# Holding the value and output weights behind the query and key weights of the second group

## The chip, the cores and the metric

The kernel runs on one core of a Trainium2 chip. The metric is the device time of one execution in microseconds (us). The core has five instruction streams that matter here: TensorE (PE, with its weight loads PEld) multiplies and transposes, VectorE (DVE) and ScalarE (ACT) move results out of the accumulator memory (psum) and do the elementwise work, GpSimd (POOL) does small copies, and SyncE (SP) issues all DMA transfers. Each stream runs its instructions in the order in which they were written and waits on semaphores for the others.

## The reference

Two layers, each a memory-augmented attention (A) and then a gated MLP (B), over 2048 tokens of width 448; both layers use the same weights. Attention walks over 64 segments of 32 tokens; 8 memory rows go in front of each segment and come out of it changed, so the segments form a recurrence.

```python
for s in range(n_seg):                       # 64 segments, one after the other
    h = concat([mem, x[:, s*32:(s+1)*32]])   # 8 + 32 rows
    q, k, v = h @ Wq, h @ Wk, h @ Wv         # 16 heads of 256
    p = softmax(where(mask, q @ k.T / 16, -1e9))
    o = sum_over_heads((p @ v) @ Wo)
    mem = o[:, :8]; outs.append(o[:, 8:])
# B: (relu(x @ W_gate) * (x @ W_up)) @ W_down
x = x + A(layernorm(x)); x = x + B(layernorm(x))   # twice
```

## The kernel before, in words

The kernel first folds weights: for each head A = Wq·Wkᵀ (scaled) and B = Wv·Wo, both kept in on-chip memory, so that the later work is per head a product with A, a softmax and a product with B. Folding needs the weights turned: TensorE transposes a loaded piece into psum (L742 for Wq and Wk, eight matmuls a turn; L747 for Wv), DVE or ACT copies it into one of seven buffers `WT`, and TensorE multiplies (L761).

The heads' query and key weights come in four groups, g = 0 to 3. Each group has four loads (query and key, two pairs of heads, here q0, k0, q1, k1), eight turns (each load has two halves, here called T30k1 for group 3, first half, k1) and fourteen products in two blocks of seven (A30, A31). There are only eight staging slots, so the loads of group 2 wait until group 0 has been turned, and those of group 3 until group 1 has. The loads of group 0 are cut in halves of 224 KB; the others have 448 KB.

Then there are eight loads of Wv (three transfers each, into slots 8 to 15) and eight of Wo. Half of Wv and Wo are folded at once (`values(0)`), half after the recurrence has gone two steps (`values(1)`). The first two steps work with unfolded Wv and Wo (`unfused`, L1039 and L1062) and need all of both.

The recurrence (`chain`) has 70 steps: layer 1's 63 and layer 2's, which follow 7 steps behind. A step multiplies the memory `mT` with A (L934), takes the softmax (`middle`), multiplies with B (L973), and turns the result into the next `mT` (L996 and L444). The attention of the other tokens (L1274, L1300, L451) and the MLP (L1372, L451) lie between the steps.

Every piece of work is an operation with its inputs and outputs, handed to a list scheduler (`_Sched`). Three things set the order: the dependencies; for SP, DVE, ACT and POOL a due time, shifted for each part of the program by a letter of the string `ORDER` (`part()`, a quarter step a letter, negative before the letter a); and for TensorE the string `LINE`, which picks in turn from the operations left, so that TensorE's order is fixed entirely by it. Where the scheduler's own clock expects TensorE to be idle for long, it puts in filler matmuls (L1406, a line of `spin`). An operation reads `r`, writes `w`; a name in `r` is waited for. DMA number n also waits for number n − 48.

## Time and profile before

| | us |
|---|---|
| median of 3 runs | 1504.0 (1503.89 to 1506.61) |
| profiled execution | 1502.79 |
| its span, first to last instruction | 1501.0 |
| granted TensorE clock, mean | 0.999 |
| TensorE busy | 1482.8 |

| stretch (us) | what it is |
|---|---|
| 0 to 62 | weights arrive and are folded; the recurrence begins at 57.55 (L934) |
| 62 to 100 | the first two steps with unfolded Wv and Wo (L1039 at 67.87 and 85.64), the rest of the folding |
| 100 to 1501 | recurrence, attention and MLP together; the MLP's weights are issued from 87.5 to 162.5 |

The profile gives each instruction's start and length; "idle before" is the time that its engine stood still ahead of it, and the arrow names the event that ended it. The granted clock is the share of full speed that TensorE's throttle let through.

### The profile page before, as it was taken

What the parts mean: (1) busy time and instruction counts of PE and PEld (TensorE: products, weight loads), DVE (VectorE), ACT (ScalarE), POOL (GpSimd) and SP (SyncE); (2) the same over time, 40 slices, a digit from 0 to 9 for tenths busy, and PEclk for the clock granted to TensorE, in tenths of its full rate; (3) what the DMA queues carried; (4) which work ended last, traced back from release to release, by engine and by line L of the source; (5) the groups of instructions that cost most, each with busy time, mean ns of one, the idle gap of its engine ahead of it and who ended that gap; (6) DMA issues with size and microseconds to landing.
All of it is one profiled execution on the core that took longest, in us unless ns stands there. A gap on an engine that the chain in (4) does not pass through costs nothing.

```text
span 1501.0 us, 83432 instructions
## 1 busy us (share of the span) xinstructions
PE 1482.8 (99%) x37128; PEld 1059.1 (71%) x37128; DVE 1144.8 (76%) x3528; ACT 909.7 (61%) x2539; POOL 171.7 (11%) x669
## 2 busy tenths in 40 slices
PE   8999999999999999999999999999999999999999
PEld 6557566676767777777768677777768776677776
DVE  6657678787777878688878877688777877778765
ACT  6776566666666666555565656565665665565543
POOL 3010111111111111011110111011110011111000
PEclk9999999999999999999999999999999999999999
DMA  9602100000000000000000000000000000000000
GB/s 231 184 25 66 54 7 12 11 9 8 9 4 12 11 8 15 4 17 6 17 6 12 11 9 14 3 18 5 18 5 8 14 9 14 4 10 6 12 5 15
DMA packets 62262, 34.12 MB, mean 23 GB/s; under 512 B 31552, under 2 KB 61776, under 8 KB 61904
## 3 DMA queue, kind: packets, MB, share of 16 engines
q1 hardware_dynamic: 61904, 28.80, 8.1%
q8 instruction: 292, 4.78, 1.4%
q14 instruction: 66, 0.54, 0.1%
HBM read 21.36 MB, written 1.84 MB: 15 GB/s over the span
## 4 chain that ended last, share of the span: by engine, by line
PE 94%; DVE 2%; ACT 1%; DMA 1%; issue 1%; SPq 0%; POOL 0%; DVEq 0%
PE psG L451 24%; PE psG L1274 17%; PE psG L1372 12%; PE psC L973 11%; PE psC L934 9%; PE psG L934 4%; PE psG L1185 3%; PE psG L761 3%; PE psG L1300 2%; PE psC L451 2%; PE psC L1128 2%; PE psC L1185 1%; PE psG L973 1%; PE psG L1188 1%; DMA Bsb<-in_A_Wq_dram 1%
## 5 line engine op out<-in xcount | busy, mean ns | idle before, releaser
L1274 PE MATMUL psG<-HT,A 64*128 64x128 bf16 x4980 | 288.9, 216 | 1.2 <-issue 1.2
L451 PE MATMUL psG<-Bsb,YT 128*128 128x448 bf16 x1288 | 274.6, 352 | 0.0
L1274 PE MATMUL psG<-HX,A 64*128 64x128 bf16 x3735 | 269.6, 216 | 0.5 <-issue 0.3
L1274 PEld LDWEIGHTS psG<-HT,A 64*128 64x128 bf16 x4980 | 236.5, 94 | 13.6 <-issue 4.2
L441 ACT ACTIVATE Ug<-psG 64x128 bf16<-64x128 f32 (+2 forms) x442 | 156.6, 374 | 68.5 <-PE psG L1274 56.6
L1274 PEld LDWEIGHTS psG<-HX,A 64*128 64x128 bf16 x3735 | 195.5, 94 | 0.8 <-issue 0.8
L1372 PE MATMUL psG<-G,glu 64*128 64x128 bf16 x5950 | 190.7, 216 | 1.2 <-issue 0.9
L1372 PEld LDWEIGHTS psG<-G,glu 64*128 64x128 bf16 x5950 | 175.4, 94 | 13.6 <-issue 6.2
L451 PEld LDWEIGHTS psG<-Bsb,YT 128*128 128x128 bf16 x1288 | 113.0, 97 | 95.7 <-issue 10.0
L973 PE MATMUL psC<-Bsb,YTm 128*32 128x448 bf16 x3416 | 172.9, 353 | 0.4
L1112 DVE STREAM_TRANSPOSE uT<-Usb 128x384 bf16<-128x384 bf16 x280 | 154.0, 551 | 0.8
L934 PE MATMUL psG<-A,mT 64*32 64x448 bf16 x4032 | 152.5, 350 | 0.0
L934 PE MATMUL psC<-A,mT 64*32 64x448 bf16 x3808 | 147.3, 350 | 0.5 <-ACT mT L441 0.5
L973 PEld LDWEIGHTS psC<-Bsb,YTm 128*32 128x32 bf16 x3416 | 85.5, 97 | 67.0 <-DVE YTm L444 1.6
L441 ACT ACTIVATE YT<-psG 128x448 bf16<-128x448 f32 x233 | 118.8, 543 | 10.6 <-PE psG L1188 9.1
L444 DVE CAST Ug<-psG 64x128 bf16<-64x128 f32 (+2 forms) x254 | 108.1, 438 | 16.9 <-PE psG L1274 12.9
L934 PEld LDWEIGHTS psC<-A,mT 64*32 64x32 bf16 x3808 | 76.0, 92 | 53.4 <-ACT mT L441 5.2
L1377 ACT ACTIVATE hG<-psG 128x512 bf16<-128x512 f32 (+1 forms) x127 | 69.0, 543 | 63.2 <-PE psG L1372 58.0
L451 PE MATMUL psG<-glu,hG 128*128 128x448 bf16 x448 | 99.3, 352 | 0.0
L934 PEld LDWEIGHTS psG<-A,mT 64*32 64x32 bf16 x4032 | 80.1, 92 | 19.8 <-DVE mT L444 0.7
L1378 DVE TENSOR_TENSOR hG<-hG,psG 128x512 bf16<-128x512 bf16 (+1 forms) x116 | 70.5, 613 | 29.2 <-ACT hG L1377 28.3
L444 DVE CAST YT<-psG 128x448 bf16<-128x448 f32 x136 | 82.0, 616 | 9.5 <-PE psG L1188 8.1
(235 smaller groups left out, 2856.9 us busy)
## 6 DMA issues: line engine op xcount, KB each, us to landing
HR<-xn SPq DMA_DIRECT2D x128, 32.0 KB
Tsb<-Rsb SPq DMA_DIRECT2D x256, 1.5 KB
Tsb<-Rsb SPq DMA_DIRECT2D x256, 2.0 KB
Bsb<-in_A_Wk_dram SPq DMA_DIRECT2D x6, 448.0 KB
Bsb<-in_A_Wq_dram SPq DMA_DIRECT2D x6, 448.0 KB
HR<-Rsb SPq DMA_DIRECT2D x126, 1.5 KB
HR<-Rsb SPq DMA_DIRECT2D x126, 2.0 KB
X<-in_A_x_dram SPq DMA_DIRECT2D x16, 112.0 KB
```

The costliest lines, as they stand in the source:

```text
L441: return E.activation(out, i, ACT.Copy, scale=1.0 if scale is None else scale)
L444: return E.tensor_copy(out, i)
L451: return E.matmul(out, lhsT=lhsT, rhs=rhs, **k)
L761: i = E.matmul(bk.ap()[row0:row0 + mn, to:to + of.stop - of.start], lhsT=lhs[:, et, m0:m0 + mn], rhs=rhs[:, et, of], start=(et == 0), stop ...
L934: i = E.matmul(ub[v].ap()[32 * j:32 * j + 32, 0:D], lhsT=self.mT[rw, WHERE[b], first:first + 32], rhs=cols, start=(b == 0), stop=(b == 6), ...
L973: x = E.matmul(bo.ap()[32 * j:32 * j + 32, 0:D], lhsT=self.YTm[:, q, :], rhs=self.Bsb[:, chunks[q], :], start=(i == 0), stop=(i == 13), ti ...
L1112: self.s.add("dve", 578, lambda E, e, out=out, hh=hh: E.transpose(out, heads[hh]), r=[("Usb", 2 * half + v) for v in range(2)], w=[f"uT{ha ...
L1185: return E.matmul(ps[:, n * q:n * q + n], lhsT=HR[rows, 128 * q:128 * q + 128], rhs=PT, start=True, stop=True, tile_position=(b, 0))
L1274: i = E.matmul(ub[v].ap()[:, 128 * n:128 * n + 128], lhsT=self.A[rw, b, a0:a0 + 128], rhs=HT[rw, WHOLE[b], :, 0:SEG] if CROSS[b] is None e ...
L1372: i_ = E.matmul(two[v].ap()[:, 128 * c:128 * c + 128], lhsT=self.Wgu[rw, b, f0:f0 + 128], rhs=G[rw, WHOLE[b] if CROSS[b] is None else 4 + ...
L1377: s.add("act", 170 + 0.833 * N, lambda E, e, dst=dst, z=two[0], N=N: E.activation(dst, z.ap()[:, 0:N], ACT.Relu), r=[two[0]], w=[("hG", i, ...
L1378: s.add("dve", dv_cost(N), lambda E, e, z=two[1], N=N, dst=dst: E.tensor_tensor(dst, dst, z.ap()[:, 0:N], ALU.mult), r=[two[1]], w=[("hG", ...
```

## The change

Three edits. First, each turn of query and key weights and of Wv counts itself and writes a name with its number, `("turned", n)`; the program adds the eight turns of a group one after the other, so number 16 is the last of group 1, T11k1. Second, every load of Wv and Wo reads `("turned", 16)`, so SP waits for that turn before it issues any of them. Third, `ORDER` and `LINE` are new strings of the same number of parts and operations.

```diff
-ORDER = ("AkAPMPZMEsWPzkVtwAm0YgdLXFCHdymsALTpcTXKWNMRKLt0H0AgHAG0gihNl0bCLbZBRyVqwoWAgOvEFplk0ptQ0orawUuaBIdaABka0AA0aa"
+ORDER = ("UmAPMPKcivEldPoriUbRkLTLNJGAf0xHXdoenVpAhHQfNEWvukAQBufSjhHCW0EXWAwAauKAwp0BxPPAAfdpsqrPwpYakozaLnIavdcaYoO0aa"
...
-LINE = ("AFGEENLEGEEEFEEEMIIFGFEEFFMEM~UIJHEEEEAEDGAGECCCCCECABIIICFBECCBBKJCDCEDCBCBJJIECFDDBBJMrBIMNIAEBCECCACADBaaCC"
+LINE = ("AEEFEMMEJHHGEEEEHGGEFEGGEEELLLHJFEFEEEAM~JLIGEFEEDDDKKEFDEFDDADAKBCBFBCBBACKBAIDABCABANBIAMNHECJADDCBAAcFBAZZB"
...
             self.dma(self.Wst[slot][:, 0:3, :], src[64:448, c0:c0 + 512].rearrange("(k p) c -> p k c", p=128), 393216,
-                     w=[("Wst", slot)])
-            self.dma(self.Wst[slot][0:64, 3, 0:256], src[0:64, c0:c0 + 256], 32768, w=[("Wst3", slot)])
-            self.dma(self.Wst[slot][64:128, 3, 256:512], src[0:64, c0 + 256:c0 + 512], 32768, w=[("Wst4", slot)])
+                     r=[("turned", 16)], w=[("Wst", slot)])
+            self.dma(self.Wst[slot][0:64, 3, 0:256], src[0:64, c0:c0 + 256], 32768, r=[("turned", 16)], w=[("Wst3", slot)])
+            self.dma(self.Wst[slot][64:128, 3, 256:512], src[0:64, c0 + 256:c0 + 512], 32768, r=[("turned", 16)], w=[("Wst4", slot)])
 
         def transposes(slot, hh, wt, rot):
             s.part()
+            turn[0] += 1
...
-            s.add("pe", ..., fn, r=keys + ["ident"], w=[bk], alloc=[bk], room=[("WT", wt)])
+            s.add("pe", ..., fn, r=keys + ["ident"], w=[bk, ("turned", turn[0])], alloc=[bk], room=[("WT", wt)])
...
-                self.dma(self.Wos[n][:, :, :], self.Wo_d[:, 4 * p:4 * p + 4, :], 458752, w=keys + homes[n])
+                self.dma(self.Wos[n][:, :, :], self.Wo_d[:, 4 * p:4 * p + 4, :], 458752, r=[("turned", 16)], w=keys + homes[n])
...
-                    self.dma(self.Wos[n][hh], ..., 229376, w=[keys[hh]] + homes[n])
+                    self.dma(self.Wos[n][hh], ..., 229376, r=[("turned", 16)], w=[keys[hh]] + homes[n])
```

Read against the order in which the program adds the operations, the two `LINE` strings give TensorE these orders up to the first step (Tg-half-load is a turn, A and B blocks of products, n0 and n1 the first tiles' transposes, U0 the first product of the recurrence, "mask" small setup matmuls):

```
before: T00k0 T00k1 T00q0 T00q1 T01q1 T01q0 A00 T01k0 T01k1 T10k0 A01 T10q1 T10k1 T11q0 T10q0 T11q1 n0 A10 mask
        T11k1 T11k0 A11(1) mask A11(6) T20q0 T20k1 T20k0 mask T20q1 T21q0 T21k0 T21q1 A20 T21k1 T30q1 T30k0 A21
        T30k1 T30q0 T31k0 T31q1 T31q0 A30 Tv00 Tv01 n1 T31k1 B00 B01 Tv10 B00 mask A31(3) B00 A31(3) B01 A31 B10 B0 U0
after:  T00q0 T00k0 T00k1 T00q1 T01k0 T01q1 A00 T01q0 T01k1 A01(6) T10k0 T10q1 A01(1) T10q0 T10k1 T11q0 T11k0 T11q1
        A10 T11k1 mask T20q1 n0 T20k0 A11 T20q0 T20k1 T21q0 T21k0 A20 mask T21k1 mask T30k0 T21q1 A21 mask
        T30k1 T31k0 T30q1 T30q0 T31q1 A30 Tv01 T31k1 Tv00 T31q0 B01 Tv10 B00 A31(2) B0 A31(2) B00 A31(3) B00 n1 Tv11 B01(2) U0
```

In the loads' part of `ORDER`, the first tile's x load goes from the letter A (6.5 steps early) to U (1.5 early). Group 1's loads stand at q0 0.75, k0 −3.75, q1 −0.75, k1 −5.25 before, and at −1.75, −3.75, −3.25, −4.25 after; group 3's at 0.25, −6.0, −3.75, 0.25 before, and at −5.5, −0.75, −1.0, −6.5 after (in steps, negative is earlier).

More of the change, by code (lines that the diff above doesn't have):

```diff
@@ L32 @@
 STEPS = "ABCDEFGHIJKLMNOPQRSTUVWXYZabcdefghijklmnopqrstuvwxyz0"
-ORDER = ("AkAPMPZMEsWPzkVtwAm0YgdLXFCHdymsALTpcTXKWNMRKLt0H0AgHAG0gihNl0bCLbZBRyVqwoWAgOvEFplk0ptQ0orawUuaBIdaABka0AA0aa"
-         "UaWkSa0fNaChwaA0kcaaXrwSQNQolVYPjLmRRyjDqc0uzbiwvY0gEaaatIahC0NHXvgHbX0qAhiALw0iY0xVfRVDkaUymAt0AaAYaeCfRWpXfR"
-         "lJxhempFZBlhCipGXOTk0eOorF0OaAa0faVtHTAdPi0SgiUZl0Nm0FmTRpXckrAguNAAk0TxnnA0HxlDgNSEoEVUlUXDaSSAHiaEFaPPSQjusW"
-         "YsHcogi0CaBoAdNDtXVPMQkFMca0pUUVDgiUJ0xagIaPQboIbArY0SqePoFsAwfZKMgAmQsVlzU0HCASKQgeTRjtIFHqamOut0D0ya0nLcrAeT"
-         "qrItxafza0hRCbp0ClsrvyAbvP0nD0EOIc0PZVUvetwAYKgbvL0w0KalaAOavpQIi0oAA0ZoAYlwmSPsLHUKDArMgzAgUELIXQA0LdqAnU0duA"
-         "RSfhqzjm0kXOhRXJVfMAtVaKbaPYaKxc0G0ZSzTNpcOgMoKsBXiXfRmvsXAophduABSMYerUaaYlanAPrjhwGfrKHNc0WWgiNONAY0ZjIihT0V"
-         "t0QqJhnS0LcxVbFjWBImEg0GMxNQjpxcpwkS0I0aYzavtOoz00gKAX0cLJkCaCWwVoVlVNmZ0jObxAFx00DReqAnTgacYaA0VBQTGgvXdZNTGn"
-         "ixZZaanneAvXk0qXyH0tAXRAocegRGeXokpA0bAxdEZoHCsFcPcys0oFa0raAmeZcEyZQprpBkgUf00mVmuQAL0tfAtAILpMjffkzbZy0UJaXD"
-         "aDgXWPdp0AXdVewhBXaIvATytDudIpyJxp0XTUswAFVsNGsiaRpOZz0ZRPojkrzZQnAfLhuKvaKXa0yCmDasEGHmoHFQXN0bYLZLTJDiANQTbR"
-         "BwmtqZMtPAyNaPhavEUjupByVrFRkoAjhqSSfsUwC0AXoNBSmwAPyyXOpAcrWU0SeRJ0EpypIhQsmOFtmBji0vczampgaOqCxa0Zj0AAYMaaaa"
-         "aavRbLKjCaaaaaaaaaaaaaaaaaaawkgqnN0IaIleHbO0")
@@ L45 @@
-SIGNS = "ABCDEFGHIJKLMNOPQRSTUVWXYZabcdefghijklmnopqrstuvwxyz0123456789+-*/=<>()[]{}.,:;!"
-LINE = ("AFGEENLEGEEEFEEEMIIFGFEEFFMEM~UIJHEEEEAEDGAGECCCCCECABIIICFBECCBBKJCDCEDCBCBJJIECFDDBBJMrBIMNIAEBCECCACADBaaCC"
-        "TPAnCCASCAQhAPDAONAgMBAKBAAHbHCGADaACCAAHIAVAYGBADOADCLCADJOFAHOEONEFGEBACCFBBCAAAAWAAAKARAAHOdHASAZAQXEAAAB~D"
-        "AK~BAffDAC=CbAEAYEDW5WWWAAETADDRQAAANAAAKKKAJJAIAHHABFAADACAAAAAAAMSYYBAKdKbKAMR~JXAMLA~NAAAEEAHDAaaFFCCGCUABB"
-        "RACPAANNNOAALANwMA1LJCJIICLHHHAGJIAAEFLAADCCAAAAABABAMAAXXQHJAaIIAQAVAAASDFDACDCbbFABADCAETAAXRABPBANNNAALANM4"
-        "4MKRArKIIIBHHHAGAIHeAADEAACBBFAAAABCAATMBAXWdWKAaKhJALWuALbKAAAEJEUADDA55ElECG0ABBxBwAdCBssstAEApArqDOCAmkBBKQ"
-        "hmAfVe+eeeCIdcAdcHCQAFAVVAGZAARAPIOhENNNANALMALLKcAaDIAAPGBaFZBEEEFAACKEPyxW~QEUEtAGAAPoBsnA~BDCkkkAAiiDADCgfA"
-        "ADAbABBXdAAVAUAXTTTATzSBBwRQCBAAMARAAJDIAHHHKAHGBSGGdAFOTZPgOAADATNBXNBfLBBBRFFBEAAF))GqpFA/BBlF9=A8L777AA5AI5"
-        "5BtBiF0AA4yDvAAttcCrrrAagEEA=FlkFlkDDhZngNACCcAbCaaaBZbAbaBFAEAVAAEQXRAPWPcDDNNNAALNKK-+aZK7ADA+4Vl2DMCzzzFAAI"
-        "wvUETDssACApACtABBjADhAAfCBEcccAcAaABaZCvBWAVAAZASuSlsARRRBCAANAbhAAKAAsriiWJBBUHHAFPAREAAaABRfBL1LBBBFFBIEB))"
-        "HSGACCAF+BBB7ACe4B7A222FbAAyAxzynewCAcCBGpguoTGFRkEQiiiESEEeAVcDccD7ibjAAZYsYDXXXBWABHWVHAlTAQAWgAPANUNpCMMMAA"
-        "KMDIAH44UDTC0GAQA2wDD~KuTDssstAAqYEApoEDlMAAiADmAfDCdAADaaaAAYABAYXAAAUSxpZTARsRCBBANNNOAALAYACIAAGBRWdGFAPYOE"
-        "AAATNBYBWgLBBBbIBEAAH{]MCCC>}RCADC-BEA8hE666AA4A55AbA2AAyCy3BwwedCVArrrGqFsrEeADPmDjDDoiRDffDKUcccfAAbaEaaHBBB"
-        "VHATZAKAQAEDVNTNNNAALA//AIABGH7NG5AA3KRA000QJyACwzyDTCSuAKApDvpANnm!CCkkkAEAhDDAFAAbccDDAAAXAAVAUTnTTTATqiECBB"
-        "OBAAAAYelAjXKAAIIkASRATGAACACSNCWMBdBBBFFBOEHAA))SGpF=CCCAE9LA7oDD4445AA2AA0E10ZygxAAeXtks:CvAqqqIgFBEAkADlkCF"
-        "iCLmCdeCKcEaDCGXXXABVAXXUAUABSAABGOASNTMaMMMAAUJJJKQ77ff5D+AA2GB0AAyyyDAAvAxwAAKJsYpAAoHBMlk>CBiiijEAAfAAAAedA"
-        "aCABBWWAAATYAStSSSAphBAAOBcAooDaAAkdApoAWvWuZJVVhHBGHGRAQPFAAACNaABMttLBBBFFJBEEBAC76DnmDAHBiy4BBwBY~LAtkDCqqq"
-        "~CqVpCAAonEECkAAoBhgNAeDKcccAAbaIAaZAXOBVHFcZLSGAQqFPPPAHDMDZLNMGbKDJAAAGLTGZBFFFAAGACAAwwCVCLsFABBoCCBqEkAJii"
-        "iAIPCeAgfBBbA[aaDAeAXBBVAUUUAASARTSqpZSAtQBPAOAAMMMNAAKAAdWrBBGGSmSdGGAZPFBQBDaTODNACCCGGCFCHT][ITHq<ADA*HAB=A"
-        "8K7778AJA4A54dlBBA6ayAAwAvultttwuAAbrFpaoFponBFEkqEEE8hoElgYjHeeeGdfFeeE,AmHDYgZDDXPDaEUTaDWSSSAXRAYY-vEPdWAAU"
-        "DMSOCQQQAERANAMDCNNAAAKIAAHFAEEADDDUADCAQBAUcGTGGRHAGBADRAEADDGAAJBOBCCBEAADCAAAAAACAAADAAAABAAAAAA")
@@ new lines @@
+ORDER = ("UmAPMPKcivEldPoriUbRkLTLNJGAf0xHXdoenVpAhHQfNEWvukAQBufSjhHCW0EXWAwAauKAwp0BxPPAAfdpsqrPwpYakozaLnIavdcaYoO0aa"
+         "aaWcAaUVxaaIpaAlY0aai0Y0ZNAjTVwPoQ0FEyVIq0fuSZvpzA0vkaaamBasfFDFXkoYut00DkF0L0heIdxbda0OTazVKZrSAaGoa0DOtHpViK"
+         "PGxcveYjZgpkkgpAqlaLseF0uTzZGgaHsaTikaSdktz0Zim0iXBmeYiIJpFWHIzRkNKwexT0mqTTBGlfzPCho0U0bIXL0eGJRqaxYaHPBPqugL"
+         "nWHcGUCrWas0XoED0MmYJRTFbDTzWUHkTcxUFrzacOaASSIdbBAFnOqWfxShAAm0RbgFhXzEJTN0GRH0Kz0Au0jUyDAcs0ouD0IXlarvNjzAtK"
+         "IX0iHadka0mbaUpuMzcmvkSRq00uM0jGIsiPzcOoeWiAwKgtaelzsIapahpaY0MAd0bAFkXoFekcgSnVTBKKQORijun0Uny0XQVIKokAfqYtuD"
+         "AkfJueUU00wAuOXPleXPaAaWAafgAXjcoWbhTzQG0fYgEcabHX0EKWHXYXl0apVuiT0foyRV0ajDa0IqlXhtOrUVHYl0gOgRHWvUYrAlbAZSfV"
+         "gmetJPaAeAclvhAfvbXmAEZHOxAszfhcfebAajgar0akcGai0AoANp0QTM0UaDW0TtV0yde0xQOfhylx0qAKp0LtMZairaHxPHATdZKliZBNMB"
+         "txkyZqJnZNwNzYwQygX00XS0PkPgUAXAGkAg0RaYnHZrVA0DcCSgXitSar0aDTcUbEn0GfRpcAXc00SDMQ0QakEsOUxASGcLkfgf0rWVZdRarI"
+         "aKPSzpdrAZVMVAcQAAa0CYPEtofBdrPvApSAYTsokf0cNFjjsTdATzfTQAKjngAeYnylJUlTeaXaaavrVTaxbAmdonGuvp0CnemcTABZWFskbu"
+         "bsORqqA0WexLadNa0dA0tpadzKqRJiBYJqLqD0cwSr0hS0CUmEABwyjrfEVra0fFaX00PAAfthNkOUJtAl0Whe00aijDaJch0R0rHFGVFCaaaa"
+         "aaQrAVKpOaaaaaaaaaaaaaaaaaaahiQkANCxaoLstbYO")
@@ new lines @@
+SIGNS = "ABCDEFGHIJKLMNOPQRSTUVWXYZabcdefghijklmnopqrstuvwxyz0123456789+-*/=<>()[]{}.,:;!"
+LINE = ("AEEFEMMEJHHGEEEEHGGEFEGGEEELLLHJFEFEEEAM~JLIGEFEEDDDKKEFDEFDDADAKBCBFBCBBACKBAIDABCABANBIAMNHECJADDCBAAcFBAZZB"
+        "AANVBBOSBhRAAQACNAhMAAKBAAHcBGBFDAaOCCBAHXAGAGXBADOADCLCADPJFAHOENNEFGEAACCFBBCAAAAWAAAKARAAHOdHASAZAQEWAAAB~D"
+        "BAJD!feD<DAbFAAYAXD5CVVVFAASADCQPAAAMAAKKKAJJAIAIHABFAADACAAAAAAAMSZYBAKdKbKAMR~JXALLA~NAAAEEADGAaaGFICCCUABBR"
+        "WABPAANNNAALAKMvLA0KCPJIICHHHAHGIHAAFLAADCCAAAAABAAAMAAXXQHAIaJIAQAVAAASGDBCABBBaaEBADCFATAARAQBBARNNNAALANM44"
+        "MKRArKIIIBHHHAGAHHeAAFDAACBBAEAAABCAAMSAAXWdAJUaKhJYMAuMAbKAAAKEEATDA76nGFCC1GABB3xBAvdCBssstAAqArqCACBMlBBRiK"
+        "AgfVeeeCCcHAadcGAAENAWAAKRSEWAPjPrPPPAANNANNNBeAVLDAPAIPHHaaCBFFFAHACCQJyx~RFUUEtAGAwAPoAEm~BDlllAFAiAAAfBBeeA"
+        "DADCAYAdAWAVUCASSSA1SRASRAPAANAAAAJDIAHHHIKdAGBTZHHddAQGiPPAXACDANBBhLLUBBBRFFBEHAA[)FpFoC/CGC+Aj/8AKE555AAH32"
+        "A32Ahzq5yAACvAzBtcsssAiAqEADmXFcAiiC5CgmABBdiKBbCeaaaBZAYZYGBFAbUAAARADPdEUDNNNAALLKLE99ZYJ6*AAm3VC1MCzzzAEAIv"
+        "vEDSsSrrAAAPunDAABBiEADDeAFcccAAaAbbyCCAWXAAAATwwSSmWARRRBCAANAAAZAeJBsjiWJBAHHSiRAFAEAVAOCAXNfBdLzBBBFFBEHB(("
+        "HGDACC-AEBK/7ADe4CAA111FaAAyxAyxmdv1ABbiBGGoSeXkTERhEgggEgADdDDccD7zFaAAhYdXXBWWWBWIUAUUmIHAAIPAAeASMLpLRLLLMA"
+        "AJAJH44VUDC0AA4EPwD~LvUDDsssaAAEpoApoEmDMAAiEAAfCCdhAcccAAaABABAYXVAAATpwSARWsRABBANNNAAMLAAXAAAHTYBFdGFAOYOEA"
+        "AATNBiBXLLBBBRaBQEBI{]DDSACQ=CDDAFB8/A7gE555AA3A243AaA0AAyfxweXyBAsssBAEqpDepoEDclDDDinDggDfffKAOfcATccDBGBFVW"
+        "AAAAEXAQDOVOUDNNNAALAK/*ACHAH=7CNBLE2EA0EOyyyOHwAvxwTTtCArKQBAnCAl!CBjjjkADACCFAdcAdcDDAAAXAAVaAUTmTTTBAphABAA"
+        "AMAhAAYkCAWHIATGcGGhQAAEAPUACAMWBLdBBBFFJBEALA[)GqRF=CCG(CA9LA7oED444AA22A32jbzAyaAAv0eCjs,jAqqqBFBEAFkAPijjHC"
+        "CgCCCdcKEaCHCXXXCaAVAUGWVACAARAANFNSMBbLRLLLAUDJLIQ87ffD4A9GA1FBzZEAwwwAAuAtvuBAJJqwAABGmASjj=BAhhhiAABeABAdcD"
+        "AZCCAAVAaATAStSSSAphBAAOOBBaoAmAYkAcpYCBVAtGGSUBRGFQaAPEAALABMRZBwMuLBBBFFoJQBEEEBA65EmDk8CHzCABwfBzuA~IDCrrr~"
+        "CrBBAppFeCClACNiCmgNBeDKcccAJbaAAZZYPCAVFMcZGSARrGFPPPEPANDNNeMWFDKAAOAHUCGZBFFFIAAACAAAwvBUBKrBJBCnsWmAMCBiii"
+        "EAIAeAffAcAA[aaDAeAXCBVAUUUAUASATSqpSAXtQBPAOAAMMMNAAKAXdABqBGGSmSdGGAZPFBWcQEBDNAMCCCMGGCFC]]ItHT>EAB[/AG-AM9"
+        "99AA7A6AI65BdBkFbAyAA52wAvultttAtcHrIppAFnonAEErksEEiES5AfXeeeFFdgcEeeDa.ciDZGDDDWOaVUEbXDSSSTAXRFAXX+uXAANUZD"
+        "MSOCQQQFSAANAMCCONLAAAJAAHFAEEADDDUACCABPfIBAFAQQEAVENEGAGFCCAAKEBEDBLBBACACBEGAAAAAAADAAADBAAAAAA")
@@ L748, in fn @@
                 return i
-            s.add("pe", mm_cost(*[128 if slot >= 8 else 112] * 8), fn, r=keys + ["ident"], w=[bk], alloc=[bk], room=[("WT", wt)])
+            s.add("pe", mm_cost(*[128 if slot >= 8 else 112] * 8), fn, r=keys + ["ident"], w=[bk, ("turned", turn[0])], alloc=[bk], room=[("WT", wt)])
             s.add(EV, ev_cost(896, fast=True), copy_any(T.rearrange("p a b -> p (a b)"), lambda: bk.ap().bitcast(BF)[:, base:base + 896]),
@@ L765, in product @@
             s.add(EV, ev_cost(D), copy_any(dst, lambda: bk.ap()[:, 0:D], scale), r=[bk], w=w)
-        wt = [0]
+        wt, turn = [0], [0]
         def nw():
@@ L812, in weights @@
                 for hh in range(2):
-                    self.dma(self.Wos[n][hh], self.Wo_d[:, 4 * p + 2 * hh:4 * p + 2 * hh + 2, :], 229376, w=[keys[hh]] + homes[n])
+                    self.dma(self.Wos[n][hh], self.Wo_d[:, 4 * p + 2 * hh:4 * p + 2 * hh + 2, :], 229376, r=[("turned", 16)], w=[keys[hh]] + homes[n])
             for k in homes[n]:
```

## Prediction

> **What bounds the kernel now.** I read the page's busy shares and its chain first.

> ```profile
> span 1501.0 us, 83432 instructions
> PE 1482.8 (99%) x37128; PEld 1059.1 (71%) x37128; DVE 1144.8 (76%) x3528; ACT 909.7 (61%) x2539; POOL 171.7 (11%) x669
> PE 94%; DVE 2%; ACT 1%; DMA 1%; issue 1%; SPq 0%; POOL 0%; DVEq 0%
> ```

> TensorE is busy 99% of the span, and 94% of the chain that ended last is TensorE. It runs its instructions in the written order, so time is to be had only where it stands idle, runs slowly, or does filler. The idle time in all is 1501.0 − 1482.8 = 18.2 us. Next I asked where it lies, with the table by stretches (columns: length, then busy us of PE, PEld, DVE, ACT and POOL, granted clock, DMA share, GB/s).

> ```profile
> 20.00:30.00 10.00, 8.92 (x141) 6.49 (x141) 6.87 (x15) 7.21 (x14) 0.32 (x1) 1.00 1.13 244
> 30.00:40.00 10.00, 7.50 (x140) 6.49 (x138) 6.11 (x17) 6.52 (x10) 0.00 (x0) 0.95 1.11 267
> 150.00:200.00 50.00, 48.03 (x1172) 32.30 (x1156) 36.13 (x108) 28.78 (x80) 5.59 (x21) 1.00 0.15 42
> 200.00:400.00 200.00, 197.93 (x5073) 137.04 (x5072) 157.75 (x513) 129.47 (x377) 27.95 (x110) 1.00 0.05 10
> 400.00:1000.00 600.00, 599.13 (x15551) 436.90 (x15549) 474.20 (x1490) 360.94 (x1049) 66.12 (x264) 1.00 0.05 10
> 1000.00:1400.00 400.00, 398.65 (x10337) 289.67 (x10333) 312.93 (x997) 242.12 (x700) 44.36 (x179) 1.00 0.05 10
> 1400.00:1501.00 101.00, 98.05 (x2276) 70.26 (x2260) 65.68 (x181) 45.49 (x120) 4.25 (x17) 1.00 0.04 10
> ```

> The 1200 us from 200 to 1400 hold 2.07 + 0.87 + 1.35 = 4.3 us of idle time. The single stretch from 30 to 40 us holds 2.5 us, and it is the one place here where the granted clock falls. There the weights are still arriving. I took that place in steps of 2 us, and then TensorE in order of time (start, length, what; in brackets the idle time before and who ended it).

> ```profile
> 34.00:36.00 2.00, 2.00 (x45) 1.51 (x42) 1.70 (x4) 1.54 (x5) 0.00 (x0) 1.00 1.12 237
> 36.00:38.00 2.00, 0.75 (x16) 0.59 (x12) 1.45 (x9) 1.31 (x3) 0.00 (x0) 1.00 1.12 260
> 38.00:40.00 2.00, 0.75 (x9) 0.78 (x9) 0.00 (x0) 0.00 (x0) 0.00 (x0) 0.75 1.11 330
> 40.00:42.00 2.00, 2.00 (x13) 0.89 (x13) 0.63 (x1) 0.98 (x2) 0.00 (x0) 0.50 1.10 356
> 42.00:44.00 2.00, 2.00 (x20) 0.95 (x16) 1.24 (x2) 1.26 (x3) 0.00 (x0) 0.90 1.11 315
> 60.00:62.00 2.00, 2.00 (x46) 1.49 (x26) 2.00 (x6) 1.84 (x4) 0.46 (x2) 1.00 0.76 194
> 62.00:64.00 2.00, 2.00 (x20) 1.25 (x18) 1.97 (x5) 2.00 (x4) 0.41 (x2) 1.00 0.11 34
> ```
> ```profile
> 15.96 2.84 PE L761 MATMUL psG<-glu 128*64 128x448 bf16 x28
> 20.81 1.34 PE L742 MATMUL psG<-ident,Bsb 112*128 112x112 bf16 x24 [1.12 <-DMA Bsb<-in_A_Wq_dram]
> 25.38 0.95 PE L742 MATMUL psG<-ident,Bsb 112*128 112x112 bf16 x16
> 35.79 0.96 PE L742 MATMUL psG<-ident,Bsb 112*128 112x112 bf16 x16
> 39.25 0.90 PE L742 MATMUL psG<-ident,Bsb 112*128 112x112 bf16 x8 [2.50 <-issue]
> 40.19 3.91 PE L761 MATMUL psG<-glu 128*64 128x448 bf16 x28
> 44.03 2.15 PE L742 MATMUL psG<-ident,Bsb 112*128 112x112 bf16 x40
> 48.95 1.07 PE L747 MATMUL psG<-ident,Bsb 128*128 128x128 bf16 x16
> 67.87 0.29 PE L1039 MATMUL psC<-Bsb,YTm 128*32 128x256 bf16 x2
> ```

> L742 turns query and key weights, eight matmuls a turn; L761 multiplies them into A; L747 turns Wv. At 39.25 TensorE has waited 2.50 us for one turn. The row says "issue", so the profile names no releaser. No engine works meanwhile (38 to 40 us: DVE, ACT and POOL all 0.00), and DMA is full, so I read it as a weight that had not landed. By the written order it is a key weight of the last group, g = 3. After it the clock is 0.50, and the same 28 products take 3.91 us that took 2.84 at 15.96. Third, the queue of SP, which issues all loads:

> ```profile
> 13.05 5.35 SPq L706 DMA_DIRECT2D Bsb<-in_A_Wv_dram  x3
> 24.95 0.32 SPq L706 DMA_DIRECT2D Bsb<-in_A_Wq_dram  x1
> 25.31 2.98 SPq L706 DMA_DIRECT2D PTx<-in_A_mem_dram  x5
> 28.34 0.32 SPq L706 DMA_DIRECT2D Bsb<-in_A_Wk_dram  x1
> 29.12 0.32 SPq L706 DMA_DIRECT2D Bsb<-in_A_Wq_dram  x1
> 29.49 0.61 SPq L706 DMA_DIRECT2D Bsb<-in_A_Wk_dram  x1
> 30.14 0.75 SPq L706 DMA_DIRECT2D glu<-in_A_Wo_dram  x1
> 30.93 4.23 SPq L706 DMA_DIRECT2D Bsb<-in_A_Wv_dram  x3
> ```

> Exactly one Wv load (three transfers, at 13.05) goes out ahead of the four loads of group 3. Everything else of Wv and Wo is already behind them. That is all that the new hold can move.

> **The change part by part.** (a) *The wait at 39.25.* The hold takes one Wv load from in front of group 3: by the code 393,216 + 2 × 32,768 = 458,752 bytes. At the 237 to 260 GB/s of 34 to 38 us that is 1.8 us, so the last group lands about 1.8 us earlier. The new table also changes who waits. It asks for one group-3 turn (a key) ahead of the products at 40.19, where the old one asks for two; behind those products it has five turns, which between them need all four loads of the group. The work ahead of these five is what was done by 36.75 (39.25 − 2.50) plus 2.84 of products, so TensorE reaches them at 39.6 if nothing stops it. If the key that landed at 39.2 was the one issued at 28.34, two loads (0.92 MB) follow it; at 330 to 356 GB/s they land near 41.9, now at 40.1: a wait of 0.5 us. If it was the one issued at 29.49, all is there by 37.4 and nothing waits. The other bound is the old row at 44.03, which did not wait: landing at 44.0, now 42.2, a wait of 2.6. I take 0.5, so this saves 2.0 us (bounds −0.1 to 2.5).

> (b) *The clock.* With a short wait the slow stretch goes: 3.91 − 2.84 = 1.07, and the slow turn 0.90 − 0.48 (half of the row at 35.79) = 0.42; together 1.5 us. It returns if the wait ahead of the five turns is long, since 2.50 idle us behind two turns were enough here.

> [...]

> (c) *The first two groups.* The new table puts key turns earlier and postpones the first tile's x load. At 20.81 the old order waits 1.12 us for the last query weight of group 1, and the new one asks for that weight one turn (0.48) earlier, with five turns of the group from there on instead of three. The landing sets both. Zero, between −0.6 and +0.6.

> (d) *The hold itself.* Wv and Wo wait for turn 16, the last of group 1, in the old trace within the row at 25.38, so until about 26.4. SP issues in order; behind such a wait stand the copies of the normed tiles, the memory pieces and the rest of Wv and Wo. The old queue had 2.98 us of memory pieces at just that time, and the group-3 loads ask for turns of the same group, so SP stands there anyway: zero. The first user of Wv is the row at 48.95, now near 45.4. A load issued at 31 lands near 42 if it takes the 10.9 us from 28.34 to 39.25: zero behind 3 us of cover. If another Wv and Wo go ahead of it (0.92 MB, 3 us at 330 GB/s), that cover is gone, and more would cost 0 to 3 us.

> (e) *The end of the loads.* The bytes are the same, and transfers fade at 62 us (194, then 34 GB/s). Step 0 needs all of Wv at the row at 67.87, now near 64.4: cover of 2.4 us, zero, at worst 1.5.

> (f) *The rest of the order.* Read against one another, about two thirds of the places in the table of TensorE's order change, mostly by one or two places. Nothing in the trace prices that; its nearest rows are the idle times from 150 us on (1.97, 4.3, 2.95). I take zero, bounds −4 to +8, the upper one below.

> Sum: −2.0 − 1.5 = −3.5 us. The profiled execution took 1502.8 us with its span of 1501.0, 1.2 below the median of the runs (1504.0). So 1499.3 for a like execution and **1500.5** against the median.

> **The rivals.** *The wait moves.* The five turns wait 2.6 us, the clock falls again, and only small change is left: 1503.5. For it: all four loads are needed within 2.2 us. Against it: less stands ahead of them.

> *The hold moves nothing that counts.* The waited-for key went out at 28.34, behind 2.98 us of memory pieces; if its issue and not the queue ahead set its landing, the bytes moved do not matter: 1504.

> *More than the start.* The reorder also removes idle time behind 62 us, of which 150 us on alone shows 9.2: four of them give 1496.5.

> *The recurrence gets longer* (slower). Each step's products of the memory with A wait for the memory's last copy:

> ```profile
> 705.84 0.93 PE L451 MATMUL psG<-glu,hG 128*128 128x448 bf16 x4
> 709.20 0.44 DVE L444 CAST mT<-psC 64x48 bf16<-64x48 f32 x2
> 709.87 1.07 PEld L934 LDWEIGHTS psG<-A,mT 64*32 64x32 bf16 x56 [0.37 <-DVE mT L444]
> ```

> The copy ends at 709.64 and the next step's weights load at 709.87: 0.2 us of slack. A four-matmul pass like that at 705.84 (0.93 us), put one place too early ahead of a link of this chain, costs 0.93 − 0.23 = 0.7 us in that step. By the code there are 70 steps (63 and a lag of 7). Five of them cancel (a) and (b), which is where the sign turns; ten add 3.5 to that: 1507.5; sixteen give 1512. For it: the order changes along the whole table and the slack is small. Against it: most moves are one or two places, and many cross nothing of the chain.

> **How the numbers follow.** A measurement of this kernel can tell about 0.2%, 3 us, from no change. Forecast 0.40 (its own range 1498 to 1502.5, of which 0.28 lies under 1501), more than the start 0.18, the wait moves 0.12, nothing moved 0.04, longer recurrence 0.26. Faster: 0.28 + 0.18 = 0.46. Same: 0.12 + 0.12 + 0.04 = 0.28. Slower: 0.26. The range 1493 to 1510 takes in (f) on both sides and leaves out the far halves of the second and the last case.

> **What would show it.** Right: no Wv issue ahead of the last query or key issue on SP; no 2.5 us of idleness between 30 and 44 us, clock 1.00 there, 28 products in 2.84 us; the first Wv turn (48.95) some 3.5 us earlier; idle time from 200 to 1400 near 4.3 us. Wrong: idleness of over 2 us ahead of the 40-matmul group of turns with a clock under 1.00 behind it; a wait at L747 or L1039 for a DMA; or idle time at L934 and L451 in the long stretch well above 4.3 us.

## The result, and the profile after

| | before | after |
|---|---|---|
| median of 5 runs on one chip | 1504.0 us (1500.78 to 1506.62) | 1498.19 us (1497.33 to 1500.39) |
| after / before | | 0.996, 95% interval 0.9941 to 0.9978 |
| profiled execution | 1502.79 us | 1497.44 us |
| its span | 1501.0 us | 1495.7 us |
| first step begins (first row of `chain`'s product, L934 before, L935 after) | 57.55 us | 53.37 us |

The kernel after is 5.8 us faster between the medians and 5.35 us between the two profiled executions. The forecast was 1500.5 us (1493 to 1510), faster by 3.5. Line numbers from L742 on are one higher in the kernel after.

The page of the kernel after, its spans and the record of the instruction queue, which the prediction left out (packets, MB, share of 16 DMA engines):

```profile
span 1495.7 us, 83407 instructions
PE 1480.7 (99%) x37123; PEld 1057.4 (71%) x37123; DVE 1140.5 (76%) x3523; ACT 920.6 (62%) x2552; POOL 170.6 (11%) x661
q8 instruction: 292, 4.78, 1.3%
PE 95%; DVE 2%; DMA 1%; SPq 1%; ACT 1%; issue 0%; POOL 0%; DVEq 0%
```

The stretches of the kernel after (columns as in the prediction):

```profile
30.00:40.00 10.00, 9.29 (x153) 7.21 (x154) 6.16 (x12) 7.54 (x13) 1.35 (x1) 1.00 1.13 291
150.00:200.00 50.00, 48.17 (x1238) 32.79 (x1238) 34.41 (x111) 30.50 (x86) 6.45 (x24) 1.00 0.10 29
200.00:400.00 200.00, 197.68 (x5039) 137.37 (x5040) 159.86 (x518) 125.86 (x374) 27.28 (x108) 1.00 0.05 10
400.00:1000.00 600.00, 598.91 (x15495) 435.17 (x15490) 470.30 (x1472) 369.02 (x1063) 66.24 (x263) 1.00 0.05 10
1000.00:1400.00 400.00, 399.79 (x10488) 291.31 (x10485) 314.60 (x1002) 247.82 (x703) 44.51 (x179) 1.00 0.05 10
```

From 30 to 40 us TensorE is idle for 0.71 us instead of 2.50, and the granted clock is 1.00. From 200 to 1400 us the idle time is 2.32 + 1.09 + 0.21 = 3.62 us, 0.67 less than before. TensorE in order of time:

```profile
14.43 2.46 PE L762 MATMUL psG<-glu 128*64 128x448 bf16 x24 [0.27 <-DVE glu L444]
18.95 2.14 PE L743 MATMUL psG<-ident,Bsb 112*128 112x112 bf16 x40 [0.67 <-DMA Bsb<-in_A_Wq_dram]
34.98 0.57 PE L762 MATMUL psG<-glu 128*64 128x448 bf16 x4 [0.27 <-DVE glu L444]
36.00 2.46 PE L762 MATMUL psG<-glu 128*64 128x448 bf16 x24 [0.45 <-issue]
38.43 2.13 PE L743 MATMUL psG<-ident,Bsb 112*128 112x112 bf16 x40
41.73 2.91 PE L762 MATMUL psG<-glu 128*64 128x384 bf16 x56 [0.89 <-DVE glu L444]
44.57 0.62 PE L748 MATMUL psG<-ident,Bsb 128*128 128x128 bf16 x8
53.37 1.52 PE L935 MATMUL psC<-A,mT 64*32 64x448 bf16 x56
```

The five turns at 38.43 wait for nothing, the first Wv turn comes at 44.57 instead of 48.95, and 24 products take 2.46 us at a granted clock of 1.00. One row will turn out to matter most: the block A21, 28 products that need no new load within them, is broken after four of them by a stall of 0.45 us with no releaser. SP's queue:

```profile
20.34 1.11 SPq L706 DMA_DIRECT2D Bsb<-in_A_Wq_dram  x2
21.49 1.80 SPq L706 DMA_DIRECT2D Bsb<-in_A_Wk_dram  x1
27.02 0.58 SPq L706 DMA_DIRECT2D Bsb<-in_A_Wk_dram  x1
29.70 0.41 SPq L706 DMA_DIRECT2D glu<-in_A_Wv_dram  x1
```

The four loads of group 3 are out by 27.6 us, and the first Wv load follows them. In the traces' landing events the last load of group 3 lands at 38.93 us before and at 35.24 after.

Step by step, from the start of each step's first product of the memory with A in the two traces: after is 4.2 us ahead at step 0, 3.4 at step 5, 5.4 at step 69, the last; the tail behind it is equally long. So the start gave 4.2 us, steps 0 to 5 took 0.8 back, and steps 5 to 69 gave 2.0.

### The profile page after: what moved, and what is told of

Same layout as the page of the kernel before. It is cut to its first block, busy times and chain, and to the rows that moved or that the text cites. A ratio compares the mean times of both kernels' runs of the same rounds, so it can differ in the third digit from the quotient of the medians.

```text
span 1495.7 us, 83407 instructions
## 1 busy us (share of the span) xinstructions
PE 1480.7 (99%) x37123; PEld 1057.4 (71%) x37123; DVE 1140.5 (76%) x3523; ACT 920.6 (62%) x2552; POOL 170.6 (11%) x661
## 3 DMA queue, kind: packets, MB, share of 16 engines
q8 instruction: 292, 4.78, 1.3%
HBM read 21.36 MB, written 1.84 MB: 16 GB/s over the span
## 4 chain that ended last, share of the span: by engine, by line
PE 95%; DVE 2%; DMA 1%; SPq 1%; ACT 1%; issue 0%; POOL 0%; DVEq 0%
PE psG L451 25%; PE psG L1275 17%; PE psG L1373 12%; PE psC L974 11%; PE psC L935 9%; PE psG L935 4%; PE psG L1186 3%; PE psG L1301 3%; PE psG L762 2%; PE psC L451 2%; PE psC L1129 2%; PE psC L1186 1%; PE psG L974 1%; PE psG L1189 1%; DMA Bsb<-in_A_Wq_dram 1%; SPq L706 1%
## 5 line engine op out<-in xcount | busy, mean ns | idle before, releaser
L451 PE MATMUL psG<-Bsb,YT 128*128 128x448 bf16 x1344 | 286.9, 352 | 0.0
L451 PEld LDWEIGHTS psG<-Bsb,YT 128*128 128x128 bf16 x1344 | 117.8, 97 | 98.1 <-issue 10.0
L935 PE MATMUL psG<-A,mT 64*32 64x448 bf16 x3976 | 151.5, 350 | 0.5 <-ACT mT L441 0.5
L935 PE MATMUL psC<-A,mT 64*32 64x448 bf16 x3864 | 148.8, 350 | 0.2 <-issue 0.2
L444 DVE CAST Ug<-psG 64x128 bf16<-64x128 f32 (+2 forms) x276 | 110.9, 412 | 16.0 <-PE psG L1275 10.7
L935 PEld LDWEIGHTS psC<-A,mT 64*32 64x32 bf16 x3864 | 76.3, 92 | 54.0 <-ACT mT L441 3.3
L451 PE MATMUL psG<-glu,hG 128*128 128x448 bf16 x434 | 96.0, 353 | 0.0
L935 PEld LDWEIGHTS psG<-A,mT 64*32 64x32 bf16 x3976 | 78.9, 92 | 20.1 <-ACT mT L441 1.7
L444 DVE CAST YT<-psG 128x448 bf16<-128x448 f32 x130 | 78.5, 614 | 13.6 <-PE psG L1189 13.1
```

What stands on the lines that cost most here:

```text
L444: return E.tensor_copy(out, i)
L451: return E.matmul(out, lhsT=lhsT, rhs=rhs, **k)
L935: i = E.matmul(ub[v].ap()[32 * j:32 * j + 32, 0:D], lhsT=self.mT[rw, WHERE[b], first:first + 32], rhs=cols, start=(b == 0), stop=(b == 6), ...
```

## The experiments

The theory at the outset is the prediction's: TensorE at 39.25 waits for a key weight of group 3, the hold brings it forward, and the later part of the order does nothing. The first runs take the change apart, the later ones ask what TensorE waits for. The runs came in three lots (e1 to e4, e5 to e8, e9 to e11), each on another chip and with its own runs of the kernel before, whose medians were 1503.75 us (35 runs), 1502.91 (34) and 1503.92 (25).

**The parts of the change alone.** e1: the old strings with the hold (edits one and two of the change).

> The kernel before with the hold alone: its ORDER and LINE stay. SP's queue differs from before in one thing, the first Wv load now stands behind the four loads of group 3. Theory (bytes ahead of group 3 set its landing): the wait of 2.50 us ahead of turn T30k0 shrinks to about 0.7 (1.8 us less), the clock stays at 1.00 between 38 and 44 us, and the first product of the recurrence (U0, 57.55 before) starts near 54.2; time 3 to 3.5 us under before. Rival 1 (the key's own issue at 28.34 behind the memory pieces sets its landing): wait and U0 as before within 0.5 us, time the same. Rival 2 (the new order did it, not the hold): also as before.

e2: the new strings without the hold (`r=[("turned", 16)]` taken off the loads).

> The changed kernel without the hold: its ORDER and LINE stay, Wv and Wo may go out at once. In SP's queue 1.31 MB of Wv and Wo (one Wv, one Wo, the large part of a second Wv) now stand ahead of the last loads of group 3. Theory (bytes ahead of group 3): 1.31 MB at about 0.25 MB per us is 5 us, part of it behind work: a wait of 2 to 5 us between 20 and 40 us, a slow clock behind it, U0 at 56.5 to 59 instead of 53.4, time at or above that of the kernel before. Rival (order alone): U0 within 0.7 us of 53.4, time as the changed kernel.

e3: the hold, and the new strings only up to the first step.

```diff
-ORDER = old                 LINE = old
+ORDER = new[:110] + old[110:]   LINE = new[:153] + old[153:]
```

> Hold, and the new strings for the start alone (LINE's first 153 places, ORDER's first 110 parts); behind that the strings of before. Theory (four fifths of the gain is made by the first step): U0 at 53.4, last step's start (1434.1 before, 1428.7 after) near 1430, time 4.2 us under before and 1.1 above the changed kernel. Rival (the rest of the order carries the gain as well or more): time within 2 us of before.

e4: no hold, the old strings up to the first step and the new ones behind it. e5 is the same with the hold.

```diff
-ORDER = old                 LINE = old
+ORDER = old[:110] + new[110:]   LINE = old[:153] + new[153:]
```

> No hold, the strings of before for the start, the new strings behind it (LINE from place 153, ORDER from part 110). Theory: U0 as before at 57.5 with the 2.5 us wait, time 1.1 us under before. Rival (the new rest is worth more by itself): 3 us or more under before.

> The hold, the old strings for the start (LINE to place 153, ORDER to part 110), the new strings behind. The hold alone measured -3.5 us and the new rest alone -3.2 us. Theory (the two are separate: hold acts on the start, the new rest on steps 5 to 69): they add up, 1497.1 or within 1 us of it, so at least as fast as the changed kernel, and the new start strings are worth nothing. Rival (they overlap: the -3.5 of the hold alone is not from the start but from how the rest falls out): 1499.5 to 1501.

With these ran the kernel after once more (e6) and the kernel before once more with a profile (e8).

> The changed kernel once more, unchanged, beside the others on their chip. Time 1498.2 within 0.7; granted clock 1.00 in the start, U0 between 53 and 55, steps 5 to 69 taking 1283.6 within 1 us if the rest is the same from run to run.

> The kernel before once more, unchanged, for a second profile of it. If the start is set by when weights land, U0 differs by 0.5 to 3 us from 57.55 and the difference reaches the end; if the rest is the same from run to run, steps 5 to 69 take 1285.6 within 0.5 us.

| kernel | hold | start | rest | median us (runs) | ratio, 95% interval | step 0 begins | gain at step 0, 5, 69 |
|---|---|---|---|---|---|---|---|
| before | no | old | old | (see above) | | 57.55 | 0, 0, 0 |
| e8, before again | no | old | old | 1503.91 (8) | | 55.51 | 2.0, 0.7, 1.1 |
| e1 | yes | old | old | 1500.29 (11) | 0.9975, 0.9961 to 0.9988 | 57.49 | 0.1, 0.7, 2.3 |
| e3 | yes | new | old | 1502.33 (11) | 0.9988, 0.9974 to 1.0002 | 54.93 | 2.6, 0.3, 0.0 |
| e4 | no | old | new | 1500.57 (12) | 0.9983, 0.9967 to 0.9999 | 60.88 | −3.3, −3.6, −2.7 |
| e5 | yes | old | new | 1501.41 (12) | 0.999, 0.998 to 1.0 | 55.01 | 2.5, 1.7, 3.6 |
| e2 | no | new | new | 1502.67 (11) | 0.9987, 0.9972 to 1.0002 | 58.75 | −1.2, −2.8, −0.9 |
| e6, after again | yes | new | new | 1498.1 (11) | 0.9975, 0.9963 to 0.9987 | 54.02 | 3.5, 2.9, 5.7 |

The last column is in us against the first profile of the kernel before. Each ratio is against the lot's own runs of the kernel before, and it is not the quotient of the two medians. Alone, e3 is not clear of noise and e4 hardly. The hold (e1, −3.5 us) and the rest (e4, −3.2), added up, would have put e5 near 1497 (0.9975 times 0.9983 is 0.9958), and it took 1501.41 (0.999, 0.998 to 1.0).

Four things follow:

- First, the kernel before itself begins its first step at 55.51 or at 57.55 us: a single profile carries 2 us of chance, and against the second one the two profiles of after are ahead by 2.1 and 1.5 us at step 0, not by 4.2 and 3.5.
- Second, the parts do not add: with the hold, the new start alone makes 1500.29 into 1502.33 under the old rest, but 1501.41 into 1498.1 under the new one.
- Third, the hold alone (e1) and the whole change run again (e6) have the same ratio, 0.9975 (0.996 when it was first measured), so these runs do not show that the new order as a whole adds anything to the hold. The hold's gain has the size that was expected, but not the place: e1's first step begins at 57.49 us, as before, and in its profile 1.6 of the 2.3 us come behind step 5; no run shows why.
- Fourth, the new order needs the hold. Without it (e2) the first step begins at 58.75 us, 4.7 to 5.4 later than in the two profiles of after. By the medians, each against its own lot, e2 gains 1.1 us and e6 4.8, though their intervals overlap.

The trace of e2 shows a wait that the hold spares, the second of these rows:

```profile
20.30 2.15 PE L743 MATMUL psG<-ident,Bsb 112*128 112x112 bf16 x40 [1.31 <-DMA Bsb<-in_A_Wq_dram]
29.31 0.55 PE L743 MATMUL psG<-ident,Bsb 112*128 112x112 bf16 x8 [1.32 <-DMA Bsb<-in_A_Wk_dram]
58.75 1.52 PE L935 MATMUL psC<-A,mT 64*32 64x448 bf16 x56
```

The turn at 29.31, T20k0, reads a load of group 2 that went out at 14.93 us, behind a load of Wv and one of Wo; it landed at 29.18, and in after at 21.59. The first row's wait is another matter: its load, of group 1, went out at 8.33 ahead of any Wv, and landed at 20.26 against 18.91 (after) and 19.68 (e6).

But where the hold stood alone (e1), the wait ahead of T30k0 stayed, 1.86 us, though the last load of group 3 landed at 35.54 instead of 38.93:

```profile
37.77 0.55 PE L743 MATMUL psG<-ident,Bsb 112*128 112x112 bf16 x8 [1.86 <-issue]
38.31 4.50 PE L762 MATMUL psG<-glu 128*64 128x448 bf16 x28
```

The load that T30k0 reads landed, by the trace's events, at 34.97 us before and at 31.94 in e1, 4.3 and 5.8 us ahead of the turn. TensorE was not waiting for it.

**What TensorE waits for.** e7 put 40 matmuls on a constant ahead of the waiting turn. They depend on nothing that is still to come, so they had to fill a wait for a weight.

```diff
+            turn[0] += 1
+            fill = 40 if turn[0] == 27 else 0        # behind turn T30q1
...
+                for _ in range(fill):
+                    i = E.matmul(bk.ap()[:, 448:512], lhsT=self.ident[:, :], rhs=self.ident[:, 0:64], start=True, stop=True)
```

> The kernel before with 40 plain 64-column matmuls of the identity, written to an unused part of the same accumulator bank, behind turn T30q1, where TensorE otherwise waits 2.5 us. The plan of all engines stays. It isolates the slow clock: the key still lands when it did. [...] Rival (the clock falls whatever stands in the wait, or the 1.5 us are taken back by the next wait for a load): time within 0.7 us of before.

Measured 1501.91 us (12 runs), ratio 0.9996 (0.9983 to 1.0009). A clock of 1.00 behind the fillers and a time 1.3 to 2 us under before had been expected; the clock was 0.50 from 37.90 to 41.31 us. The trace:

```profile
38.03 2.31 PE L751 MATMUL psG<-ident 128*128 128x64 bf16 x40 [2.25 <-issue]
40.16 0.94 PE L744 MATMUL psG<-ident,Bsb 112*128 112x112 bf16 x8
```

The fillers themselves wait 2.25 us, and the turn behind them does not wait. Whatever is missing, it is not data. Counted from the start of the trace, the stall stands behind 471 matmuls in before, e8, e1, e4 and e7. That made a new theory: TensorE has run out of instructions. The page's row of the instruction queue has 292 packets, 4.78 MB, so 16.4 KB each; 37123 matmuls over 292 packets are, as an estimate from these two rows, 127 matmuls a packet, if the queue carries TensorE's instructions alone, which no run shows. In the traces of before and after the packets from the 20th to the 280th do start 127 matmuls apart on average. The trace's record of this queue shows the third packet starting at 36.33 us in before, 2.92 us ahead of the end of the stall. Two runs tested it, both of the kernel before. e9 leaves out the 24 short filler matmuls on the identity, 23 of which stand ahead of the stall, in gaps between 8 and 40 us (not at the very start, as the expectation has it); e11 adds 24 small matmuls in an early wait.

```diff
 e9:
-        f.fn = lambda E, e: self.spin(E, bank, n, ns)
+        f.fn = lambda E, e: self.spin(E, bank, n, ns) if ns > 100 else None
 e11:
+            turn[0] += 1
+            fill = 24 if turn[0] == 3 else 0         # a turn of the first group
...
+                for _ in range(fill):
+                    i = E.matmul(bk.ap()[:, 448:464], lhsT=self.ident[:, :], rhs=self.ident[:, 0:16], start=True, stop=True)
```

> The kernel before without the row of identity matmuls (about 24) that it runs at the very start while nothing has landed; no dependency and no load changes. Theory of the instruction fetch: TensorE's stall of 1.5 to 2.6 us comes at the same number of matmuls from the start (470 or 471) as in the kernel before, so it is now 23 or 24 matmuls further on in the program: behind turn T30k0, some 16 matmuls into the 28 products that follow it, and the eight turns are no longer waited for. Rival, a weight that lands late: the stall of about 2.5 us stays ahead of T30k0's eight matmuls, which are now numbers 447 to 454. Time: both theories give 1502 to 1505, the half-clock stretch stays where the stall is over 1.8 us.

> The kernel before with 24 added matmuls of 16 columns on the identity, written after one of the turns of the first group, where TensorE waits for loads anyhow. Theory of the instruction fetch: the stall comes at the same number of matmuls from the start (470 or 471), so 24 matmuls earlier in the program: ahead of or inside turns T21k1 and T30q1, which are in no need of a late weight; 1.5 to 2.8 us long, and none of over 1 us ahead of T30k0. Rival, a weight that lands late: the stall stays ahead of T30k0, now at matmul number 494. Time 1502 to 1506 by both.

In e9 the turn T30k0 (in the group at 36.21) waits for nothing, and the block behind it is cut after 14 products:

```profile
36.21 1.35 PE L742 MATMUL psG<-ident,Bsb 112*128 112x112 bf16 x24
37.79 1.51 PE L761 MATMUL psG<-glu 128*64 128x448 bf16 x14 [0.22 <-ACT glu L441]
39.66 1.52 PE L761 MATMUL psG<-glu 128*64 128x448 bf16 x14 [0.36 <-issue]
54.63 1.52 PE L934 MATMUL psC<-A,mT 64*32 64x448 bf16 x56
```

In e11 the stall has moved the other way, into the block A20, 24 matmuls ahead of its old place, and T30k0 (the last of the 24 at 39.22) waits for nothing:

```profile
33.22 2.52 PE L765 MATMUL psG<-glu 128*64 128x384 bf16 x48
38.71 0.58 PE L765 MATMUL psG<-glu 128*64 128x384 bf16 x8 [2.97 <-issue]
39.22 1.35 PE L744 MATMUL psG<-ident,Bsb 112*128 112x112 bf16 x24
```

The number is 470 in e9 and 471 in e11 (the expectation miscounted the place in the program by eight matmuls, not the number). The stall follows the count of matmuls and not the weight; the late weight is refuted. That it is the instructions that are missing is the author's reading. It rests on the third packet, which starts 2.92 us ahead of TensorE's return in before (behind 466 matmuls) and 2.70 in after (behind 442). No run changed the fetch itself.

The times were missed. e9 was expected at 1502 to 1505 us and took 1500.36 (11 runs), ratio 0.9979 (0.997 to 0.9987); e11 took 1501.24 (8 runs), 0.9987 (0.9976 to 0.9998). In e9 the stall was only 0.36 us, since TensorE reached the same number 2.55 us later (39.30 us against 36.75), in long products, and came back only 0.41 us later (39.66 against 39.25). So leaving out 24 fillers, with no other edit, gave 3.5 us by the medians, as much as the hold alone.

e10 joins the two: the kernel after without those fillers.

> The kernel after without the same row of identity matmuls at the start. Theory of the instruction fetch: what is left of the stall (0.24 to 0.45 us in the two profiles of the kernel after) moves by 23 or 24 matmuls to the end of the block A21 or behind it, and stays under 1 us, because TensorE needs as long as before for the instructions of one fetch; the time is that of the kernel after, 1497 to 1499.5. Rival, that the row at the start keeps the clock up or spaces the first turns: the granted clock falls below 1.00 in the first 20 us or the first step begins over 1 us later, 1499 to 1501.

Measured 1500.03 us (9 runs, 1495.96 to 1500.78), ratio 0.9973 (0.9963 to 0.9983). No stall of TensorE is left at 470, and nothing is gained by that: the turns and products wait for data in its place, and the first step begins at 54.88 us. The time is not the 1497 to 1499.5 that was expected but the rival's (1499 to 1501).

```profile
35.47 0.95 PE L743 MATMUL psG<-ident,Bsb 112*128 112x112 bf16 x16 [0.58 <-DMA Bsb<-in_A_Wk_dram]
37.14 2.84 PE L762 MATMUL psG<-glu 128*64 128x448 bf16 x28 [0.72 <-DVE glu L444]
54.88 1.52 PE L935 MATMUL psC<-A,mT 64*32 64x448 bf16 x56
```

Its interval overlaps that of the kernel after, which has the lowest median of all.

## Why the prediction was right, and where it was not

The forecast held, with the right sign and 2.3 us too little. Its steps one by one:

- **(a), the wait: the gain right, its cause wrong.** The step that failed is "I read it as a weight that had not landed". The row said "issue", and nothing in the views showed a landing. The wait of 2.50 us went down to 0.45 (0.24 in e6), 2.05 saved where 2.0 was forecast; that the size agreed is luck. From the 1.54 us of the second profile of before it is 1.1 to 1.3. The last load of the group did land 3.4 to 3.7 us earlier (e1, after) and not 1.8, but TensorE was not waiting for it: the stall followed the count of matmuls, and that instructions were missing is the author's reading. In after it came to that count 1.2 us sooner (35.55 us against 36.75), and the third packet started 3.0 us sooner (33.30 against 36.33). Counted from matmul 354, 117 ahead of the stall, TensorE's work lasts longer (6.7 us instead of 6.1), and the packet starts sooner (4.47 us instead of 5.67); how much of the second is the hold's is open. The residual wait that the prediction gave to the five turns does not exist.
- **(b), the clock: right between these profiles, but it does not fall in every run.** The stretch at a clock of 0.50 is gone: 1.5 us by the rows of before. That a wait of 0.5 us would spare the clock was the author's estimate; behind the waits of 0.45 us in after and 0.24 in e6 it stayed at 1.00, and no run had the wait of 2.6 us ahead of the five turns. But of the 94 runs of the kernel before in the three lots, 42 show a mean clock below 1.000 and 52 do not; of 16 runs of the kernel after (5 and e6's 11), none does. The prediction was read from a profile with the fall. In the three lots the runs with the lower clock were 2.5, 1.9 and 0.6 us longer on average.
- **(c), the first two groups: too small.** At matmul 354 the two profiles of after are 1.8 and 1.0 us ahead of before, and the second profile of before 0.4; the bound was 0.6. The wait for the query weight of group 1 went from 1.12 to 0.67.
- **(d), (e), the hold and the end of the loads: right.** No turn of Wv (L748) and no unfolded product (L1040) waits for a transfer. The 10.9 us that (d) gave a load ran to the end of the stall; the load issued at 28.34 had landed after 6.6 us (at 34.97), while the Wv load issued at 30.93 landed at 41.20, near the 42 of the forecast. What was overlooked is the other side: the new order asks for the later groups so early that it needs the hold (e2's wait of 1.32 us ahead of T20k0).
- **(f), the rest of the order: not zero.** From step 5 to 69 the six kernels with the new rest gain 2.0, 2.8, 1.9, 0.9, 1.9 and 3.1 us on the first profile of before (after, e6, e5, e4, e2, e10), the six others with the old rest 0.4, 1.6, −0.3, −0.4, 1.0 and −0.2 (e8, e1, e3, e7, e9, e11): on average 2.1 against 0.4. So by these averages of single profiles the rest is worth about 1.7 us, inside the bounds of −4 to 8, and that would be most of the 2.3 us that were missed. Of it, 0.67 in the profile of after is idle time from 200 to 1400 us. The medians do not settle it so closely: each kernel against its own lot, the rest gives 3.4 us with the hold and the new start (e6 against e3), and −2.0 with the hold and the old start (e5 against e1). What the steps from 0 to 5 give or take changes from run to run.

The rivals: the wait did not move to the five turns; that the hold moves nothing that counts is true of the hold at T30k0 (e1's stall stayed) though not of the whole; more than the start was in it, as the third rival said, by part of its amount; the recurrence got no longer. Of what was to show it, the signs of "right" came: the first Wv turn at 44.57 against 45.4, and the 28 products at a clock of 1.00, though in two pieces with the stall between them (0.57 and 2.46 us). This is the lesson of the case: every sign agreed, and the cause was still another one, since none of the signs told a late weight from a late instruction.

## What to carry to other kernels

An idle row that ends in "issue", with no releaser, is not yet a data wait: put work that depends on nothing ahead of it, and if that work waits too (2.25 us in e7), count instructions. Here 24 more small matmuls (e11) or 23 fewer (e9) ahead of the stall moved it in the program and left it behind 471 and 470. In e9 long products ahead of that count hid most of the stall (0.36 us were left); in after, most of what was saved came with a packet that started sooner (33.30 us against 36.33). And a single profile of a kernel with such stalls is one draw out of several: two profiles of the same program here differed by 2 us at the first step, which is as much as most of the terms in the sum.
